# Two weight parts in conversion at once with a share for GpSimd, and attention normalised after the value product

## Chip, core and metric

The kernel runs on one core of a Trainium2 chip. The metric is the device time of one launch in microseconds (us). Besides the timed runs there is one profiled execution, from which every row below comes.

## What is computed

Attention over keys that are 4x4 means of `kv`, and then two feed-forward blocks one behind the other, all in float32 at the interface. The weights of the two blocks (`w_in`, `w_out`) arrive as 64-bit floats.

```python
kv_pool = kv.reshape(B, H // r, r, W // r, r, C).mean(axis=(2, 4))      # 768 keys per batch
k = v = kv_pool.reshape(B, -1, C) @ w_sr
s = scale * (q @ k.transpose(0, 2, 1)); s = s - s.max(-1, keepdims=True)
a = np.exp(s); a /= a.sum(-1, keepdims=True) + 1e-09
x = (a @ v)                                   # 2 x 12288 rows of 128
h = x @ w_in;  g = h * np.clip(h + 3.0, 0.0, 6.0) / 6.0;  x = g @ w_out     # d_ff 2048
h = x @ w_in2; g = h * np.cos(h);                         out = g @ w_out2
```

## The kernel before

**Blocks and units.** The 24576 rows are 48 blocks of 512. Per block there is one attention, and per feed-forward layer 8 units; a unit covers 256 of the 2048 hidden columns. The second layer runs LAG = 15 units behind the first, and the attention of a block is planned AHEAD = 3 units before the block's first unit.

**Precision.** Matrices are multiplied as three products of a high and a low float32r half. A unit's input pair is six matmuls of 512 columns on TensorE (lines 807 to 809), its output pair is six more (lines 815 to 817). Between them ScalarE and VectorE form the gate (line 822 then 825 in the first layer; 830, 833, 839 and 842 in the second), ScalarE rounds it to the high half (869) and GpSimd subtracts to get the low half (845). The two PSUM banks of an input pair come free when VectorE has done 825 or 842.

**Attention of a block.** The queries are transposed, by TensorE in the first BY_PE = 2 blocks (line 557, fp32), and through DRAM in the others. TensorE makes four score products (642), VectorE the row maxima (648), ScalarE the exponential with its row sums (654), VectorE one plus and one reciprocal on 128x1 (662, 665), and GpSimd scales the 768 weights of each row (669). In the first BY_PE blocks TensorE transposes the weights (725) and VectorE or ScalarE copies them out of PSUM (328, 330; the same copy helper). In the others VectorE parts the weights into 16-bit planes (697), SP stores them to DRAM (704) and loads them back transposed (740). Then come the value product (756), its high half on ScalarE (772) and its low half on VectorE (779); that pair is the input `x` of the first layer.

**Weights.** Each of the four matrices is converted from its 64-bit words in four parts, 16 in all (`plan_weight`). A part of 128x512 goes through ScalarE (358, 395) and seven VectorE operations: clamp 363, rebase 370, sign 377, power 383, rest 390, add 399, low 402. Its intermediate lies in one PSUM bank. TURNS = 1 lets one part at a time hold such a bank.

**Order.** Everything is written as operations with a priority and a planned cost; a list scheduler (`Plan.run`) picks for each free engine the ready operation with the lowest priority number and so fixes each engine's program. Weight part k of 16 has priority W_FIRST + W_STEP * k. Each engine and SP, which issues all DMAs, runs its program strictly in that order.

Of the kernel before, what the change touches and what calls it, by code (L numbers as in the profile page):

```python
# [16 lines left out]
ALU = mybir.AluOpType  # L17
# [16 lines left out]
AHEAD = 3  # L34
# [6 lines left out]
BY_PE = 2  # L41
# [3 lines left out]
TURNS = 1  # L45
# [12 lines left out]
W_FIRST, W_STEP = 10000.0, 4000.0  # L58
# [182 lines left out]
def attention_ffn_ffn_kernel(  # L241
# [45 lines left out]
    def tiles(tag, count, shape, dtype, pool=const):  # L287
# [15 lines left out]
            "scro": tiles("scro", NSCR, [C * 2, T], U16, dram),  # L303
            "scr": tiles("scr", NSCR, [NKC // 2, NJ * P * 2, 2 * P], U16, dram),
# [30 lines left out]
    def plan_weight(prio, n, src, part):  # L335
# [51 lines left out]
        def rest(e):  # L387

            t32 = work().bitcast(F32)
            nc.vector.scalar_tensor_tensor(  # L390
                out=t32, in0=words()[0], scalar=2.0**-52, in1=t32, op0=ALU.mult, op1=ALU.mult
            )
# [4 lines left out]
        def add(e):  # L397
            t32 = work().bitcast(F32)
            nc.vector.tensor_tensor(out=t32, in0=t32, in1=words()[1].bitcast(F32), op=ALU.add)

        def low(e):
            nc.vector.tensor_tensor(  # L402
                out=lo, in0=work().bitcast(F32), in1=hi.bitcast(F32), op=ALU.subtract
            )
# [8 lines left out]
        c = op(prio, {"dve": 602}, rest, [c])  # L413
        c = op(prio, {"dve": 602}, add, [c, a], drop=[raw])
        a = op(prio, {"dve": 602}, low, [c], drop=[tt, ("turn", n, part)])
# [127 lines left out]
    def plan_attention(prio, b):  # L543
# [73 lines left out]
        for j in range(NJ):  # L617
# [5 lines left out]
            scaled.append(a)  # L623
        acc, parts = ("xacc", b), []
# [7 lines left out]
        x_ready[1, b] = plan_split(prio + XS_AT, a, acc, ("x", 1, b), None)  # L632

    def plan_scores(prio, b, j, q_op, k_ops):
        ps, nm, e_, qt = ("s", b, j), ("nm", b, j), ("e", b, j), ("qt", b)
# [17 lines left out]
        def exp(e):  # L653
# [3 lines left out]
                accum_out=plan[nm][:, 1:2],  # L657
            )

        def inverse(e):  # L660
            t = plan[nm]
            nc.vector.tensor_scalar(
                out=t[:, 2:3], in0=t[:, 1:2], scalar1=1e-9, scalar2=None, op0=ALU.add
            )
            nc.vector.reciprocal(t[:, 3:4], t[:, 2:3])

        def normalize(e):
            t = flat(plan[e_])[:, 0:KEYS]
            nc.gpsimd.tensor_scalar(  # L669
                out=t, in0=t, scalar1=plan[nm][:, 3:4], scalar2=1.0, op0=ALU.mult, op1=ALU.mult  # L670
            )
# [7 lines left out]
            prio + 200, {"act": 1000}, exp, [a, *gate_exp(b)], take=[(e_, "w")], drop=[ps],  # L679
# [363 lines left out]
```

## Time and profile before

| | us |
|---|---|
| median of 3 runs | 2671.14 (2670.62 to 2671.53) |
| the profiled execution | 2667.97 |
| its span, first to last instruction | 2666.2 |

The profile gives busy time by engine, groups of instructions by line, the waits by the instruction that ended them, and a timeline. Matmuls are pipelined, so the time from one matmul's start to the next tells more than its own duration; on VectorE too an instruction's record overlaps the next by a little under 0.1 us. The granted clock is that of TensorE, 1.00 for full speed (2.4 GHz); half of that is its lower level.

### The profile page before, as it was taken

What the parts mean: (1) busy time and instruction counts of PE and PEld (TensorE: products, weight loads), DVE (VectorE), ACT (ScalarE), POOL (GpSimd) and SP (SyncE); (2) the same over time, 40 slices, a digit from 0 to 9 for tenths busy, and PEclk for the clock granted to TensorE, in tenths of its full rate; (3) what the DMA queues carried; (4) which work ended last, traced back from release to release, by engine and by line L of the source; (5) the groups of instructions that cost most, each with busy time, mean ns of one, the idle gap of its engine ahead of it and who ended that gap; (6) DMA issues with size and microseconds to landing.
All of it is one profiled execution on the core that took longest, in us unless ns stands there. A gap on an engine that the chain in (4) does not pass through costs nothing. (4 is left out here: it accounts for less than half of the span.)

```text
span 2666.2 us, 32082 instructions
## 1 busy us (share of the span) xinstructions
PE 2613.4 (98%) x11120; PEld 2064.6 (77%) x11120; DVE 2089.0 (78%) x2185; ACT 2299.1 (86%) x2613; POOL 2152.9 (81%) x1106
## 2 busy tenths in 40 slices
PE   7979999999999999999999999999999999999998
PEld 6657787778877877777777877787778777877787
DVE  8997787778777888877777777777777777777776
ACT  4888988888888888898889988998899888888887
POOL 1768888888888888788888888888888888888788
PEclk9989999999999999999999999999999999999999
DMA  6333334333433354433333343334332343234220
GB/s 191 101 84 77 87 91 104 75 88 89 105 72 91 87 139 111 111 76 89 97 83 87 78 104 85 91 75 100 91 91 72 103 92 91 72 99 91 71 60 28
DMA packets 516323, 241.77 MB, mean 91 GB/s; under 512 B 392256, under 2 KB 490688, under 8 KB 516160
## 3 DMA queue, kind: packets, MB, share of 16 engines
q1 hardware_dynamic: 516160, 239.72, 36.0%
q8 instruction: 87, 1.43, 0.2%
q14 instruction: 76, 0.62, 0.1%
HBM read 33.62 MB, written 109.31 MB: 54 GB/s over the span
## 5 line engine op out<-in xcount | busy, mean ns | idle before, releaser
L845 POOL TENSOR_TENSOR lo<-w,hi 128x1024 fp32r<-128x1024 f32 x768 | 1835.9, 2409 | 418.1 <-ACT hi L869 233.0
L869 ACT CAST hi<-w 128x1024 fp32r<-128x1024 f32 x768 | 793.2, 1051 | 111.3 <-DVE w L842 75.8
L807 PE MATMUL banks<-x,w_in_hi 128*128 128x512 f32 x1536 | 635.4, 414 | 19.5 <-DVE w L842 7.3
L815 PE MATMUL banks<-hi,w_out_hi 128*128 128x512 f32 x1536 | 629.5, 410 | 2.7 <-DVE w L825 2.3
L809 PE MATMUL banks<-x,w_in_hi 128*128 128x512 f32 x1536 | 603.1, 393 | 1.4 <-DVE x L779 1.4
L817 PE MATMUL banks<-lo,w_out_hi 128*128 128x512 f32 x1536 | 600.8, 391 | 2.2 <-POOL lo L845 2.2
L808 PE MATMUL banks<-x,w_in_lo 128*128 128x512 f32 x1536 | 602.0, 392 | 0.8 <-DVE w_in_lo L402 0.8
L816 PE MATMUL banks<-hi,w_out_lo 128*128 128x512 f32 x1536 | 599.3, 390 | 0.0
L842 DVE TENSOR_TENSOR w<-w,banks 128x1024 f32<-128x1024 f32 x384 | 465.2, 1217 | 143.9 <-ACT w L839 143.4
L825 DVE SCALAR_TENSOR_TENSOR w<-w,banks 128x1024 f32<-128x1024 f32 x384 | 462.6, 1216 | 117.3 <-ACT w L822 116.7
L833 DVE SCALAR_TENSOR_TENSOR w<-banks,w 128x1024 f32<-128x1024 f32 x384 | 466.0, 1219 | 108.4 <-ACT w L830 106.9
L822 ACT ACTIVATE w<-banks,three 128x1024 f32<-128x1024 f32 x384 | 423.6, 1118 | 43.3 <-PE banks L809 38.9
L839 ACT ACTIVATE w<-w 128x1024 f32<-128x1024 f32 x384 | 404.9, 1062 | 57.5 <-DVE w L833 55.3
L830 ACT ACTIVATE w<-banks 128x1024 int32<-128x1024 f32 x384 | 390.5, 1024 | 55.9 <-PE banks L809 53.5
L807 PEld LDWEIGHTS banks<-x,w_in_hi 128*128 128x128 f32 x1536 | 290.0, 189 | 119.4 <-DVE w L825 25.9
L815 PEld LDWEIGHTS banks<-hi,w_out_hi 128*128 128x128 f32 x1536 | 288.8, 188 | 79.0 <-issue 10.5
L697 DVE COPY w<-w 128x1536 uint16<-128x1536 uint16 x184 | 317.7, 1746 | 38.6 <-POOL w L669 38.4
L816 PEld LDWEIGHTS banks<-hi,w_out_lo 128*128 128x128 f32 x1536 | 288.8, 188 | 72.7 <-issue 17.2
L808 PEld LDWEIGHTS banks<-x,w_in_lo 128*128 128x128 f32 x1536 | 290.1, 189 | 70.1 <-issue 14.1
L809 PEld LDWEIGHTS banks<-x,w_in_hi 128*128 128x128 f32 x1536 | 289.8, 189 | 64.8 <-DVE x L779 1.8
L817 PEld LDWEIGHTS banks<-lo,w_out_hi 128*128 128x128 f32 x1536 | 288.4, 188 | 64.8 <-POOL lo L845 3.4
L756 PE MATMUL banks<-w,v_all 128*128 128x512 f32 x576 | 270.7, 593 | 0.0
(66 smaller groups left out, 1925.0 us busy)
## 6 DMA issues: line engine op xcount, KB each, us to landing
scr<-w SPq DMA_DIRECT2D x184, 384.0 KB, 2.5
w<-in_kv_dram SPq DMA_DIRECT2D x48, 256.0 KB, 5.0
w<-in_q_dram SPq DMA_DIRECT2D x48, 256.0 KB, 3.1
out_dram<-w SPq DMA_DIRECT2D x48, 256.0 KB, 2.0
scro<-w SPq DMA_DIRECT2D x47, 256.0 KB, 2.0
scrq<-w SPq DMA_DIRECT2D x46, 256.0 KB, 2.3
w<-in_moe_w_in_dram SPq DMA_DIRECT2D x8, 512.0 KB, 5.4
w<-in_moe_w_out_dram SPq DMA_DIRECT2D x8, 512.0 KB, 4.3
```

Of the source, the lines that this page charges most:

```text
L807: nc.tensor.matmul(t[:, i, :], w_hi[:, k, :], xx[:, 0, :], start=True, stop=False)
L808: nc.tensor.matmul(t[:, i, :], w_lo[:, k, :], xx[:, 0, :], start=False, stop=False)
L809: nc.tensor.matmul(t[:, i, :], w_hi[:, k, :], xx[:, 1, :], start=False, stop=True)
L815: nc.tensor.matmul(t, o_hi[:, k, :], h[:, i, :], start=(k == 0), stop=False)
L816: nc.tensor.matmul(t, o_lo[:, k, :], h[:, i, :], start=False, stop=False)
L817: nc.tensor.matmul(t, o_hi[:, k, :], l[:, i, :], start=False, stop=(k == 2 * NP - 1))
L822: nc.scalar.activation(plan[g], two(ps), AF.Relu, bias=three, scale=1.0)
L825: nc.vector.scalar_tensor_tensor(out=plan[g], in0=plan[g], scalar=6.0, in1=two(ps), op0=ALU.min, op1=ALU.mult)
L833: nc.vector.scalar_tensor_tensor(out=plan[g], in0=two(ps), scalar=0.25, in1=plan[g].bitcast(I32), op0=ALU.add, op1=ALU.subtract,)
L842: nc.vector.tensor_tensor(out=plan[g], in0=plan[g], in1=two(ps), op=ALU.mult)
L845: nc.gpsimd.tensor_tensor(out=plan[lo], in0=plan[g], in1=plan[hi].bitcast(F32), op=ALU.subtract)
L869: prio + HI_AT, {"act": 947}, lambda e: nc.scalar.copy(plan[hi], plan[g]), [a],
```

## The change

Four things at once.

1. The row sums of a block's four exponentials go to the four columns of one 128x4 tile. One plus and one reciprocal per block make their inverses. SP stores these to DRAM (`away`, 16 bytes per partition) and loads them back as one row copied to all 128 partitions (`back`). The weights stay unscaled: the 192 scalings by GpSimd (669) are gone. The value product, which has its rows along the free axis, is scaled by VectorE as it leaves PSUM; ScalarE rounds that, and GpSimd (not VectorE) subtracts for the low half (`plan_first`).
2. Two weight parts may be in conversion at once (TURNS 2), and for the first 8 of the 16 parts (`w_in1`, `w_out1`) the last two of the seven steps, add and low, are GpSimd's. The part's PSUM bank is then free after the fifth step.
3. Block 2 too is transposed by TensorE (BY_PE 3).
4. Attention is planned 4 units ahead instead of 3, and weight parts are spaced by 6000 instead of 4000 in priority.

```diff
-AHEAD = 3
+AHEAD = 4
-BY_PE = 2
+BY_PE = 3
-TURNS = 1
+TURNS = 2
+POOL_PARTS = 8
-W_FIRST, W_STEP = 10000.0, 4000.0
+W_FIRST, W_STEP = 10000.0, 6000.0
...
+        if by_pool:
+            c = op(prio, {"dve": 602}, rest, [c], drop=[tt, ("turn", n, part)])
+            c = op(prio, {"pool": 1250}, add, [c])
+            a = op(prio, {"pool": 1250}, low, [c, a], drop=[raw])
+        else:
...
-                accum_out=plan[nm][:, 1:2],
+                accum_out=plan[sm][:, j : j + 1],
...
+        def inverse(e):
+            t = plan[sm]
+            nc.vector.tensor_scalar(out=t, in0=t, scalar1=1e-9, scalar2=None, op0=ALU.add)
+            nc.vector.reciprocal(t, t)
+
+        def away(e):
+            nc.sync.dma_start(out=plan[scr].rearrange("(p j) -> p j", p=P), in_=plan[sm])
+
+        def back(e):
+            nc.sync.dma_start(
+                out=plan[row][:, 0, :],
+                in_=plan[scr].rearrange("(o t) -> o t", o=1).broadcast_to([P, T]),
+            )
...
+        def scaled(e):
+            t = plan[row]
+            nc.vector.tensor_tensor(
+                out=t[:, 1, :].rearrange("p (j q) -> p j q", j=NJ),
+                in0=one(acc).rearrange("p (j q) -> p j q", j=NJ),
+                in1=t[:, 0, :].rearrange("p (q j) -> p j q", j=NJ), op=ALU.mult,
+            )
+
+        def high(e):
+            nc.scalar.copy(plan[x][:, 0, :], plan[row][:, 1, :])
+
+        def low(e):
+            nc.gpsimd.tensor_tensor(
+                out=plan[x][:, 1, :], in0=plan[row][:, 1, :],
+                in1=plan[x][:, 0, :].bitcast(F32), op=ALU.subtract,
+            )
```

Line numbers move by up to 43. The order of the changed program differs nearly everywhere; three places follow.

VectorE while the first weight part is converted and the scores of blocks 0 and 1 come in (`w_80` is the part's raw words, `s_` the small tiles of the attention). Before:

```order
L370 TENSOR_SCALAR banks<-banks 128x512
L662 TENSOR_SCALAR s_114<-s_114 128x1
L665 RECIPROCAL s_114<-s_114 128x1
L377 SCALAR_TENSOR_TENSOR w_80<-w_80,banks 128x512
L662 TENSOR_SCALAR s_115<-s_115 128x1
L665 RECIPROCAL s_115<-s_115 128x1
L383 TENSOR_SCALAR banks<-w_80 128x512
L648 TENSOR_REDUCE s_116<-banks 128x1
L390 SCALAR_TENSOR_TENSOR banks<-w_80,banks 128x512
```

Now:

```order
L373 TENSOR_SCALAR banks<-banks 128x512
L366 TENSOR_SCALAR banks<-banks 128x512
L657 TENSOR_REDUCE s_116<-banks 128x1
L380 SCALAR_TENSOR_TENSOR w_80<-w_80,banks 128x512
L657 TENSOR_REDUCE s_117<-banks 128x1
L687 TENSOR_SCALAR s_113<-s_113 128x4
L688 RECIPROCAL s_113<-s_113 128x4
L386 TENSOR_SCALAR banks<-w_80 128x512
L333 COPY w_79<-banks 128x1024
L393 SCALAR_TENSOR_TENSOR w_80<-w_80,banks 128x512
```

One small pair stands for four, and steps of a second part (the second row) stand between those of the first.

GpSimd in the same stretch. Before, the scalings of the attention weights lead up to the first unit's low halves:

```order
L669 TENSOR_SCALAR w_79<-w_79,s_113 128x768
L669 TENSOR_SCALAR w_80<-w_80,s_114 128x768
L845 TENSOR_TENSOR lo_98<-w_89,hi_91 128x1024
L669 TENSOR_SCALAR w_79<-w_79,s_115 128x768
L845 TENSOR_TENSOR lo_99<-w_90,hi_92 128x1024
```

Now the last two steps of the weight parts do, with the low half of block 0's `x` (`x_107`) among them:

```order
L403 TENSOR_TENSOR w_82<-w_82 128x512
L407 TENSOR_TENSOR w_in_lo<-w_82,w_in_hi 128x512
L798 TENSOR_TENSOR x_107<-w_85,x_107 128x512
L403 TENSOR_TENSOR w_84<-w_84 128x512
L584 COPY w_82<-w_82 128x1024
L407 TENSOR_TENSOR w_in_lo<-w_84,w_in_hi 128x512
L403 TENSOR_TENSOR w_88<-w_88 128x512
L407 TENSOR_TENSOR w_out_lo<-w_88,w_out_hi 128x512
L887 TENSOR_TENSOR lo_98<-w_80,hi_91 128x1024
```

The scalings have left GpSimd's program and 16 weight steps have entered it ahead of the gates' low halves.

SP where a block's weights go through DRAM. Before:

```order
L704 DMA scr_128<-w_85 128x3x512
L704 DMA scr_128<-w_82 128x3x512
L549 DMA w_80<-in_q_dram 128x512
L740 DMA_TRANSPOSE w_86<-scr_128 128x2x1024
L740 DMA_TRANSPOSE w_88<-scr_128 128x2x1024
L740 DMA_TRANSPOSE w_85<-scr_128 128x2x1024
```

Now:

```order
L721 DMA scr_129<-w_86 128x3x512
L721 DMA scr_129<-w_79 128x3x512
L691 DMA scri_126<-s_114 128x4
L757 DMA_TRANSPOSE w_82<-scr_129 128x2x1024
L694 DMA w_85<-scri_126 128x512
L757 DMA_TRANSPOSE w_78<-scr_129 128x2x1024
L757 DMA_TRANSPOSE w_90<-scr_129 128x2x1024
```

The store of the inverse sums stands ahead of the three transposing loads, and the load of them between the first and the second.

## Rows read from the trace of the kernel before

**Rows 1.** The page: busy us, share of the span and instructions of each engine.
```profile
PE 2613.4 (98%) x11120; PEld 2064.6 (77%) x11120; DVE 2089.0 (78%) x2185; ACT 2299.1 (86%) x2613; POOL 2152.9 (81%) x1106
```

**Rows 2.** Busy time by stretch: PE, PEld, DVE, ACT, POOL, then PEclk, DMA share, GB/s.
```profile
34.24:60.95 26.71, 24.24 (x132) 19.70 (x133) 25.61 (x50) 18.83 (x33) 10.31 (x11) 1.00 0.25 48
60.95:100.00 39.05, 34.45 (x118) 23.54 (x118) 37.03 (x49) 29.02 (x34) 19.37 (x10) 0.91 0.43 109
100.00:160.00 60.00, 53.95 (x227) 41.92 (x225) 57.48 (x72) 53.48 (x61) 51.15 (x24) 0.98 0.31 88
160.00:220.00 60.00, 49.79 (x182) 37.03 (x183) 53.83 (x68) 45.53 (x56) 31.01 (x18) 0.91 0.29 70
220.00:2600.00 2380.00, 2371.38 (x10123) 1877.42 (x10122) 1850.16 (x1899) 2093.79 (x2363) 1986.35 (x1015) 1.00 0.37 90
```

**Rows 3.** Waits of PE, 34 to 220 us: us in total, times, longest.
```profile
PE banks L807 <- DVE w L842: 6.9, 3, 2.9
```

**Rows 4.** Timeline of DVE: start us, us, line, operation, out<-in [idle before <-releaser].
```profile
65.24 0.68 DVE L377 SCALAR_TENSOR_TENSOR w<-w,banks 128x512 int32<-128x512 int32 x1
65.83 0.15 DVE L662 TENSOR_SCALAR s<-s 128x1 f32<-128x1 f32 x1
...
66.10 0.68 DVE L383 TENSOR_SCALAR banks<-w 128x512 int32<-128x512 int32 x1
...
123.45 0.70 DVE L390 SCALAR_TENSOR_TENSOR banks<-w,banks 128x512 f32<-128x512 uint32 x1
124.18 0.70 DVE L399 TENSOR_TENSOR banks<-banks,w 128x512 f32<-128x512 f32 x1
```

**Rows 5.** DVE by line, 34 to 220 us: busy us, mean ns | idle before.
```profile
L648 DVE TENSOR_REDUCE s<-banks 128x1 f32<-128x768 f32 x17 | 16.1, 950 | 4.5 <-PE banks L642 4.4
L697 DVE COPY w<-w 128x1536 uint16<-128x1536 uint16 x8 | 14.0, 1745 | 1.0 <-POOL w L669 1.0
```

**Rows 6.** Timeline of DVE: the sixth product of the second layer.
```profile
155.38 1.22 DVE L842 TENSOR_TENSOR w<-w,banks 128x1024 f32<-128x1024 f32 x1
```

**Rows 7.** Timeline of PE: transposes of block 0's weights.
```profile
45.99 2.12 PE L725 MATMUL banks<-ident,w 128*128 128x128 f32 x16 [0.29 <-ACT w L654]
```

**Rows 8.** POOL by line, whole span.
```profile
L845 POOL TENSOR_TENSOR lo<-w,hi 128x1024 fp32r<-128x1024 f32 x768 | 1835.9, 2409 | 418.1 <-ACT hi L869 233.0 <-PE banks L817 113.4 <-issue 33.5
L669 POOL TENSOR_SCALAR w<-w,s 128x768 f32<-128x768 f32 x192 | 174.2, 916 | 44.1 <-DVE s L665 25.0 <-ACT hi L869 7.7 <-DVE s L662 5.5
L597 POOL TENSOR_TENSOR x<-w,x 128x512 fp32r<-128x512 f32 x46 | 59.9, 1302 | 5.5 <-ACT x L594 5.5
```

**Rows 9.** DMA issues: KB each, median us to landing.
```profile
scro<-w SPq DMA_DIRECT2D x47, 256.0 KB, 2.0
```

**Rows 10.** Timeline of SP, one block's transposing loads.
```profile
1269.27 6.67 SPq L740 DMA_TRANSPOSE w<-scr  x3
```

**Rows 11.** Timelines of PE, ACT and DVE: from the same block's last value product to its first unit.
```profile
1286.56 1.88 PE L756 MATMUL banks<-w,v_all 128*128 128x512 f32 x4
...
1290.01 0.68 PE L807 MATMUL banks<-x,w_in_hi 128*128 128x512 f32 x1
1290.53 0.39 PE L808 MATMUL banks<-x,w_in_lo 128*128 128x512 f32 x1
1290.76 0.40 PE L809 MATMUL banks<-x,w_in_hi 128*128 128x512 f32 x1
...
1288.47 0.59 ACT L772 CAST x<-banks 128x512 fp32r<-128x512 f32 x1 [0.59 <-PE banks L756]
...
1289.10 0.69 DVE L779 TENSOR_TENSOR x<-banks,x 128x512 fp32r<-128x512 f32 x1
```

**Rows 12.** Timelines: GpSimd continuously busy, GpSimd idle, and DVE within that idle time.
```profile
110.56 16.64 POOL L845 TENSOR_TENSOR lo<-w,hi 128x1024 fp32r<-128x1024 f32 x7 [0.59 <-DVE banks L399]
...
96.19 2.41 POOL L845 TENSOR_TENSOR lo<-w,hi 128x1024 fp32r<-128x1024 f32 x1 [12.86 <-PE banks L817]
...
91.56 0.70 DVE L399 TENSOR_TENSOR banks<-banks,w 128x512 f32<-128x512 f32 x1
```

More of the change, by code (lines that the diff above doesn't have):

```diff
@@ L390, in rest @@
             nc.vector.scalar_tensor_tensor(
-                out=t32, in0=words()[0], scalar=2.0**-52, in1=t32, op0=ALU.mult, op1=ALU.mult
+                out=words()[0].bitcast(F32) if by_pool else t32, in0=words()[0],
+                scalar=2.0**-52, in1=t32, op0=ALU.mult, op1=ALU.mult,
             )
@@ L397, in add @@
         def add(e):
[L398 to L399 removed]
+            t32 = (words()[0] if by_pool else work()).bitcast(F32)
+            ENG[e].tensor_tensor(out=t32, in0=t32, in1=words()[1].bitcast(F32), op=ALU.add)
         def low(e):
[L402 to L404 removed]
+            t32 = (words()[0] if by_pool else work()).bitcast(F32)
+            ENG[e].tensor_tensor(out=lo, in0=t32, in1=hi.bitcast(F32), op=ALU.subtract)
         a = op(prio, {"dma": 1560}, load, take=[(raw, "w")], spare=W_SPARE)
@@ L623, in plan_attention @@
             scaled.append(a)
+        row = plan_sums(prio + 1000 * NJ, b)
         acc, parts = ("xacc", b), []
@@ L678, in plan_scores, with plan_sums @@
         a = op(
-            prio + 200, {"act": 1000}, exp, [a, *gate_exp(b)], take=[(e_, "w")], drop=[ps],
-            table="exp",
+            prio + 200, {"act": 1000}, exp, [a, *gate_exp(b)],
+            take=[(e_, "w")] if j else [(e_, "w"), (sm, "s")], drop=[ps, nm], table="exp",
         )
         exps[b, j] = a
-        a = op(prio + 300, {"dve": 310}, inverse, [a])
-        return op(prio + 400, {"pool": 884}, normalize, [a], drop=[nm])
+        return a
+    def plan_sums(prio, b):
+        sm, row, scr = ("sm", b), ("row", b), ("scri", b)
+        def inverse(e):
[9 more added lines that the diff above has]
+            )
+        a = op(prio, {"dve": 310}, inverse, [exps[b, j] for j in range(NJ)], take=[(scr, "scri")])
+        a = op(prio + 100, {"dma": 500}, away, [a], drop=[sm])
+        return op(prio + 200, {"dma": 500}, back, [a], take=[(row, "w")], drop=[scr], spare=1)
     GK = NKC // 2
@@ L763, in plan_values, with plan_first @@
         )
+    def plan_first(prio, b, after, acc):
+        row, x = ("row", b), ("x", 1, b)
+        def scaled(e):
[12 more added lines that the diff above has]
+            )
+        a = op(prio, {"dve": 602}, scaled, after, drop=[acc])
+        a = op(prio + 100, {"act": 478}, high, [a], take=[(x, "x")])
+        return op(prio + 200, {"pool": 1230}, low, [a], drop=[row])
     def plan_split(prio, after, acc, x, s):
```

27 lines of the change are left out of this document (9 added, 18 removed).

## The prediction

> **What bounds the kernel now.** I read the page first, then busy time by stretch, then who ended TensorE's waits. TensorE is busy 98% of the span [rows 1], and the stretches say where the other 53 us are: between 220 and 2600 us it idles 8.6 of 2380 us at full clock, while VectorE, ScalarE and GpSimd each have over a tenth free [rows 2]. There the time is TensorE's own work, and the change takes none of that away. The loss is at the start. In the four stretches from 34.24 to 220 us TensorE idles 2.5, 4.6, 6.1 and 10.2 us, 23.3 in all. The granted clock is 0.91, 0.98 and 0.91 in the last three, below its full level behind those waits; busy time times the missing share is 3.1 + 1.1 + 4.5 = 8.7 us more. So 32 us can be won there, and half of that, 14.7, lies behind 160 us. In the same four stretches VectorE is busy 25.6 of 26.7, 37.0 of 39.1, 57.5 of 60 and 53.8 of 60 us: it carries the start, and the largest wait is an input pair that waits for VectorE's last step of the second layer [rows 3]. The first 34 us (means of `kv`) are the same in both kernels, and so is the end.
>
> **What the change takes from VectorE at the start.** Counted over the order up to the 26th first-layer gate and the 14th second-layer product, where before the last weight part is done.
> - Add and low of 8 parts: a 128x512 step occupies VectorE from 65.24 to 65.83, 0.59 us [rows 4]. 16 x 0.59 = 9.4 us less.
> - Small pairs: 16 before, 5 now. A pair takes 65.83 to 66.10, 0.27 us [rows 4]; 11 x 0.27 = 3.0 less.
> - Block 2: four plane copies fewer at 1.745 less some 0.09 of overlap [rows 5], 6.6 less; three more copies out of PSUM, which I price as the 1024-column step of 1.22 less overlap [rows 6], 3.4 more; one low half of the queries, 0.6 more. Net 2.6 less.
> - Steps that follow their own predecessor: 123.45 to 124.18 is 0.73 us instead of 0.59 [rows 4]. The order has 40 such pairs of neighbours before and 7 now, since two parts alternate: 33 x 0.14 = 4.6 less.
>
> Together about 20 us. The scaling of the product takes the place of the old low half (512 columns out of PSUM either way) and costs nothing new.
>
> **What it adds, and where it lies.** TensorE: 24 transposes of block 2 at 2.12/16 = 0.13 us [rows 7] are 3.1, four for its queries 0.5, and a few switches between fp32 and float32r (1290.01 to 1290.53 against the usual 0.23, so 0.3 each [rows 11]): 4.5 us. GpSimd: 16 x 1.30 = 21 us of weight steps and 48 x 1.30 = 62 us of low halves of `x`, against 192 x 0.916 = 176 us of scalings that go [rows 8]; it is busy 10.3 of the first 26.7 us of the start and 19.4 of the next 39.1 [rows 2], so the weight steps fit, though each part now waits for two steps of 1.30 instead of 0.59. ScalarE: at the start nothing changes but where its roundings read from; 29 scalings of the output by 0.6 us move to it from VectorE over the whole run, where both have room [rows 2].
>
> The DMAs: the trace has none of 16-byte pieces. The nearest row, 256 KB stored in runs, lands in 2.0 us [rows 9]; I take 2.0 each for `away` and `back`, with 0 (wholly covered) and 5 us each as bounds. On SP `away` now waits for the inverse ahead of the transposing loads, and `back` waits for `away` to land ahead of the second and third. One transposing load keeps SP 6.67/3 = 2.2 us [rows 10], which covers those 2.0. The three loads are issued by 1275.94 and the last value product starts at 1286.56 [rows 10, 11]: 10.6 us of cover, less landing, so even the upper bound hides. If it did not, TensorE would wait in the value product of each block.
>
> **Where the relief goes.** It does not all arrive, because the order also moves conversion forward. At the sixth product of the second layer, which ends at 156.6 us before [rows 6], VectorE has now all 96 of its conversion steps behind it instead of 82 (14 x 0.59 = 8.3 more), four more row maxima at 0.87 (3.5), three PSUM copies (3.4), one query half (0.6), one second-layer step (1.1), and nine small pairs fewer (2.4 less): 14.5 us more. Some 27 of the 33 neighbour pairs are saved by then, 3.8 us. So VectorE comes to that row 10.7 us **later** than before. TensorE has more behind it there: by the order four output pairs of the second layer (6 x 0.23 = 1.4 each), one input pair, two score products and the 4.5 us of transposes, against one input and two or three output pairs of the first layer. What is left for it is 3.5 to 10 us less than before; I take 7. From there on, before, 16.7 us are lost (the 14.7 behind 160, and 2 that I take of the 6.1 ahead of it). Now VectorE has 38 us of work up to the 14th product where before it had 52, and TensorE has over 50: TensorE leads, and only handovers cost. I take 3 us for these, between 0 and the old 16.7. Sum: +10.7 - 7 - 16.7 + 3 = **-10 us**. The extra transposes are inside the 7. Against the profiled execution that is 2668.0 - 10 = 2658; the median of the runs is 3.2 us above that execution, and the same step from it gives **2661 us**.
>
> **One rule of the skill.** VectorE's steps at 123.45 and 124.18 take 0.70 us each while GpSimd runs without a break from 110.56 to 127.2 [rows 4, 12]; the same step at 91.56 takes 0.70 with GpSimd idle for 12.86 us up to 96.19 [rows 12]. So work on GpSimd does not hold VectorE up there. The Trainium skill, Perfetto Trace Analysis, section "Optimizing Scalar/DVE Operations", warns that GpSimd and VectorE share an SBUF read port, so that moving work between the two might not help. No row shows it; its result is the fourth rival.
>
> **Rivals.**
> - *The early weights eat the relief.* TensorE waits ahead of the sixth product for what it no longer waits for behind it. For it: VectorE 10.7 us later there. Against it: second-layer work that is ready earlier. If the loss behind that row stays above 12 us, the sum is +1 to -1: 2671.
> - *More than forecast.* TensorE's remainder is 10 us smaller and no handover costs, and the early waits (13 us of idle ahead of 160) shrink too, by 6: -20, 2651.
> - *GpSimd in the chain to `x` (slower).* Before, the last value product is out at 1288.45, the low half is done at 1289.79, and its first user is the third matmul at 1290.76: 1 us to spare [rows 11]. Now the chain is 0.69 on VectorE, 0.59 on ScalarE, 1.30 on GpSimd and handovers, 2.7 us, and by the order one output pair more (1.4 us) stands between. Again 1 us to spare. But if a low half of a gate, 2.41 us [rows 8], has just begun on GpSimd, up to 1.4 us are missing. At 0.22 us a block over 45 blocks the forecast gain is gone; at 0.5 us the kernel takes 22 - 10 = +12: 2683. Against it: 394 of 2380 us on GpSimd are free [rows 2], and a planned order puts the split where GpSimd should be free.
> - *The port.* Each of GpSimd's 16 weight steps stops VectorE for its 1.30 us: +20.8 - 10 = +11, 2682. The rows above speak against it.
>
> **How the numbers follow.** Forecast 0.61, with its own range 2654 to 2667; early weights 0.17; more 0.12; chain to `x` 0.07; port 0.03. The range 2647 to 2673 holds the forecast, the first rival and half of the second. This kernel can be told from no change at about 0.2%, 5.3 us. Faster by more: nine tenths of the forecast, the second rival, little else, 0.69. Within: 0.19. Slower: the last two and a little of the first, 0.12.
>
> **What would show it.** In the changed profile: VectorE's work between 34 and 220 us lower, its sixth second-layer product near 167 us, the last weight step ahead of it; TensorE's idle time and low clock between 160 and 220 nearly gone; the stretch from 220 on at its old rate, with no wait for the scaled product or GpSimd's low half of `x`; `away` and `back` landing in about 2 us. A wait of TensorE for GpSimd in each block, or VectorE idle at the scaling, would make it wrong, as would idle time that has moved ahead of 160 us instead of vanishing.

## Result: 32 us faster, three times the forecast

| | before | after |
|---|---|---|
| median of 4 runs, us | 2671.34 (2670.62 to 2671.97) | 2639.39 (2638.53 to 2642.41) |
| profiled execution, us | 2667.97 | 2639.83 |
| its span, us | 2666.2 | 2637.8 |

The ratio is 0.9883, 95% interval 0.9865 to 0.9900. The time lies below the forecast's range (2647 to 2673), and below the second rival, "more than forecast" (2651). The page's line on the engines, after, beside [rows 1]:

```profile
PE 2599.3 (99%) x11148; PEld 2070.3 (78%) x11148; DVE 2031.0 (77%) x1852; ACT 2295.6 (87%) x2642; POOL 2055.5 (78%) x976
```

The stretches of the changed kernel, with the columns of [rows 2] (span, then busy time and instructions of PE, PEld, DVE, ACT and POOL, PEclk, DMA share, GB/s):

```profile
34.24:60.95 26.71, 23.46 (x131) 18.14 (x130) 24.59 (x38) 17.81 (x33) 7.38 (x7) 1.00 0.19 48
60.95:100.00 39.05, 32.61 (x121) 22.90 (x120) 37.60 (x50) 32.59 (x40) 33.24 (x21) 0.96 0.42 118
100.00:160.00 60.00, 58.00 (x256) 45.10 (x255) 57.98 (x75) 51.18 (x63) 46.38 (x23) 1.00 0.21 58
160.00:220.00 60.00, 59.92 (x260) 47.88 (x259) 52.03 (x47) 53.63 (x64) 43.45 (x22) 1.00 0.45 113
...
1400.00:2000.00 600.00, 600.00 (x2578) 480.90 (x2577) 455.25 (x409) 535.24 (x612) 477.93 (x225) 1.00 0.40 96
2000.00:2600.00 600.00, 600.00 (x2573) 480.19 (x2573) 451.77 (x404) 534.86 (x606) 479.65 (x223) 1.00 0.35 83
```

And the last two of these stretches in the kernel before:

```profile
1400.00:2000.00 600.00, 598.25 (x2555) 473.98 (x2555) 464.94 (x480) 530.35 (x597) 503.17 (x258) 1.00 0.36 89
2000.00:2600.00 600.00, 598.84 (x2557) 474.71 (x2556) 462.75 (x477) 528.55 (x594) 499.05 (x253) 1.00 0.34 83
```

From 160 to 220 us TensorE's idle time falls from 10.2 us [rows 2] to 0.1 and the clock is full: the forecast gain is there. But look at the steady stretches. TensorE's busy time there grows by 1.75 and 1.16 us, 0.3% and 0.2%, while the matmuls in brackets grow by 23 and 16, 0.9% and 0.6%. Something was gained that the busy column does not show.

**A measure that shows it.** Each kernel has 9216 feed-forward matmuls. The start of the 800th, and the time from there to the last, part the run into the start (with all of the weights' conversion) and the steady part. From the two profiled executions (that of the kernel before is 3.4 us below its median, that of the changed kernel 0.4 above, so the two gains add up to 28.7 us and not to 32):

| | 800th starts at | from there to the last |
|---|---|---|
| before | 316.1 | 2343.7 |
| after | 302.8 (13.3 less) | 2328.3 (15.4 less) |

The prediction forecast 10 us for the start and nothing for the steady part. So the question is where those 15.4 us come from.

**Where the steady time was lost.** TensorE in the kernel before, a first-layer input pair (start us, us, line, out<-in, idle before):

```profile
322.28 0.39 PE L808 MATMUL banks<-x,w_in_lo 128*128 128x512 f32 x1
322.50 0.40 PE L809 MATMUL banks<-x,w_in_hi 128*128 128x512 f32 x1
323.20 0.50 PE L807 MATMUL banks<-x,w_in_hi 128*128 128x512 f32 x1 [0.30 <-DVE w L825]
323.54 0.39 PE L808 MATMUL banks<-x,w_in_lo 128*128 128x512 f32 x1
```

Matmuls usually start 0.227 us apart, but each record is 0.39 long. Here a matmul starts 0.70 after the one ahead of it, since VectorE frees the bank late, and the next one 0.34 later: 0.59 us lost, of which the row shows 0.30 as idle. A stall below 0.16 us shows nothing at all. (The Trainium skill, Perfetto Trace Analysis, section "Tensor Engine Instruction (MATMUL, LD_WEIGHTS)", says that the end of a matmul in the profile is estimated from its size and not observed; the rows here show only that the records overlap.) I counted the distances over 0.25 us from a feed-forward matmul to the next one, leaving out those right behind a value product, from the 800th to the 9000th: 129 before, worth 22.2 us above 0.227, of which 8.4 show as idle; 35 after, worth 8.4, of which 4.3 show. That is 13.8 of the 15.4 us.

Who is late is mostly VectorE: of the 129, 38 (12.1 us) end within 0.2 us of a VectorE step that releases them, and 31 more (4.1 us) follow a stall directly; 2 (0.8 us) end with ScalarE, and for the other 58, all short (5.2 us), the trace names nobody. VectorE has waits of its own from 310 to 2600 us (in all, times, longest). Before:

```profile
DVE s L662 <- ACT w L654: 50.1, 78, 1.4
DVE w L697 <- POOL w L669: 34.5, 30, 2.1
```

After, the plane copies' waits:

```profile
DVE w L714 <- issue: 5.5, 32, 0.4
DVE w L714 <- ACT w L663: 1.3, 3, 0.7
```

Before, VectorE stood 50 us ahead of the small pair (waiting for the row sum of the exponential) and 35 us ahead of the plane copies (waiting for GpSimd's scaling). What stands behind them in its row, the gates that free TensorE's banks, waited too. The change takes both waits away. That alone does not explain the gain: e1 and e4 below have neither wait and keep a steady part of 2341.4 and 2340.4. Nor does VectorE wait less in total: for ScalarE at the gates (825, 833 and 842, now 867, 875 and 884) it waits 433 us where it waited 339. What counts is which gate stands behind a wait.

### The profile page after: what moved, and what is told of

Same layout as the page of the kernel before. It is cut to its first block, busy times and chain, and to the rows that moved or that the text cites. A ratio compares the mean times of both kernels' runs of the same rounds, so it can differ in the third digit from the quotient of the medians.

```text
span 2637.8 us, 32119 instructions
## 1 busy us (share of the span) xinstructions
PE 2599.3 (99%) x11148; PEld 2070.3 (78%) x11148; DVE 2031.0 (77%) x1852; ACT 2295.6 (87%) x2642; POOL 2055.5 (78%) x976
## 5 line engine op out<-in xcount | busy, mean ns | idle before, releaser
L911 ACT CAST hi<-w 128x1024 fp32r<-128x1024 f32 x768 | 781.2, 1056 | 46.7 <-DVE w L884 32.5
L849 PE MATMUL banks<-x,w_in_hi 128*128 128x512 f32 x1536 | 621.5, 405 | 9.7 <-DVE w L867 4.8
L851 PE MATMUL banks<-x,w_in_hi 128*128 128x512 f32 x1536 | 600.2, 391 | 0.0
L864 ACT ACTIVATE w<-banks,three 128x1024 f32<-128x1024 f32 x384 | 420.0, 1120 | 24.8 <-PE banks L851 24.5
L849 PEld LDWEIGHTS banks<-x,w_in_hi 128*128 128x128 f32 x1536 | 288.4, 188 | 90.1 <-DVE w L884 12.1
L850 PEld LDWEIGHTS banks<-x,w_in_lo 128*128 128x128 f32 x1536 | 288.4, 188 | 67.1 <-issue 11.4
L714 DVE COPY w<-w 128x1536 uint16<-128x1536 uint16 x180 | 310.3, 1746 | 8.1 <-issue 5.5
```

The costliest lines, as they stand in the source:

```text
L849: nc.tensor.matmul(t[:, i, :], w_hi[:, k, :], xx[:, 0, :], start=True, stop=False)
L850: nc.tensor.matmul(t[:, i, :], w_lo[:, k, :], xx[:, 0, :], start=False, stop=False)
L851: nc.tensor.matmul(t[:, i, :], w_hi[:, k, :], xx[:, 1, :], start=False, stop=True)
L864: nc.scalar.activation(plan[g], two(ps), AF.Relu, bias=three, scale=1.0)
L911: prio + HI_AT, {"act": 947}, lambda e: nc.scalar.copy(plan[hi], plan[g]), [a],
```

## Experiments

Medians of the runs; the kernel before was 2670.6 to 2671.0 beside them. "800th" and "steady" are the two columns of the table above, from each run's profile. The profiled execution of the kernel before is 3 us below its median, so the columns show less of a gain than the medians. Some expectations measure the steady part to the 9000th matmul (2292.6 before, 2277.3 after). A single profiled execution can lie some 3 us beside its median: e1's is 1.5 above.

| | us | ratio (95%) | 800th | steady |
|---|---|---|---|---|
| before | 2671.34 | | 316.1 | 2343.7 |
| after | 2639.39 | 0.9865 to 0.9900 | 302.8 | 2328.3 |
| e1 product alone | 2661.98 | 0.9954 to 0.9979 | 314.1 | 2341.4 |
| e2 weights alone | 2664.56 | 0.9969 to 0.9987 | 318.0 | 2339.2 |
| e3 AHEAD 4 alone | 2671.16 | 0.9993 to 1.0011 | 320.7 | 2342.9 |
| e4 after, AHEAD 3 | 2653.11 | 0.9921 to 0.9946 | 304.7 | 2340.4 |
| e5 product and AHEAD 4 | 2650.22 | 0.9908 to 0.9935 | 314.3 | 2328.2 |
| e6 after, BY_PE 2 | 2646.95 | 0.9897 to 0.9924 | 307.3 | 2329.5 |
| e7 after, AHEAD 5 | 2665.47 | 0.9971 to 0.9988 | 309.4 | 2345.8 |
| e8 after, no weight step on GpSimd | 2650.01 | 0.9907 to 0.9934 | 314.2 | 2328.0 |
| e9 after, small pairs back | 2660.03 | 0.9945 to 0.9970 | 311.0 | 2340.2 |
| e10 after, GpSimd's pass back | 2717.30 | 1.0159 to 1.0187 | 326.3 | 2383.3 |
| e11 after, TURNS 1 | 2655.62 | 0.9928 to 0.9953 | 322.9 | 2324.4 |
| e12 after, W_STEP 4000 | 2650.73 | 0.9911 to 0.9936 | 313.9 | 2328.5 |
| e13 after, GpSimd's pass aside | 2640.19 | 0.9871 to 0.9898 | 305.8 | 2327.1 |
| e14 e10 with AHEAD 3 | 2672.63 | 0.9997 to 1.0014 | 309.6 | 2353.7 |
| e15 after, row without a stride | 2726.98 | 1.0193 to 1.0225 | 324.3 | 2398.4 |

### The change taken apart (e1 to e5)

e1, the changed code with

```diff
-AHEAD = 4
+AHEAD = 3
-BY_PE = 3
+BY_PE = 2
-TURNS = 2
+TURNS = 1
-POOL_PARTS = 8
+POOL_PARTS = 0
-W_FIRST, W_STEP = 10000.0, 6000.0
+W_FIRST, W_STEP = 10000.0, 4000.0
```

> Only the product is normalised in place of the weights (inverse sums by way of DRAM); the weight conversion, AHEAD, BY_PE and W_STEP stay as in the kernel before. Theory A (the trace of the changed kernel shows about 16 us gained ahead of 300 us and 12 to 13 us gained little by little behind it; A says that the second share comes from the scalings that leave GpSimd and the small VectorE steps that leave the steady part, and has nothing to do with the conversion): about 12 us faster than before, near 2659, and the gain grows with the blocks, none of it ahead of 220 us. Rival B (the second share comes from AHEAD = 4, which moves the attention of a block ahead of one unit more): within 4 us of before, 2667 to 2673. Rival C (the second share comes from the late weights, whose conversion still disturbs the order): within 4 us of before too.

e2, the kernel before with the changed `plan_weight` and

```diff
-TURNS = 1
+TURNS = 2
+POOL_PARTS = 8
-W_FIRST, W_STEP = 10000.0, 4000.0
+W_FIRST, W_STEP = 10000.0, 6000.0
```

> Only the conversion of the weights is changed: two parts at once, eight parts with GpSimd's add and low, 6000 between the parts; scores are still normalised by GpSimd, AHEAD = 3 and BY_PE = 2. Theory A: the gain of the start without that of the steady part, some 12 to 17 us faster than before, 2654 to 2659, with the number of matmuls per microsecond behind 300 us as before. Rival C (conversion also gives the steady share): 25 us or more faster, 2646 or less. Prediction's reading (relief of VectorE is 20 us but the early weights eat half): 10 us or less, 2661 or more, since the pairs that the normalisation saves at the start are missing here.

e3, the kernel before with

```diff
-AHEAD = 3
+AHEAD = 4
```

> The kernel before with AHEAD = 4 in place of 3 and nothing else: the attention of a block is planned one unit earlier. Theory A: within 4 us of before, 2667 to 2675. Rival B: about 12 us faster, near 2659, by a higher matmul rate behind 300 us.

e4, the changed kernel with

```diff
-AHEAD = 4
+AHEAD = 3
```

> The changed kernel with AHEAD = 3 as before; everything else of the change stays. Theory A: within 4 us of the changed kernel, 2636 to 2644. Rival B: loses the steady share, about 2651. A third reading (the longer way through DRAM needs the unit more of lead): TensorE waits for the scaled product in each block, 0.2 to 0.5 us by 47 blocks, 2648 to 2662.

No theory fits all four. The product alone gains 9 us, but its trace shows 2.3 in the steady part where theory A wants 12. The weights alone gain 6 and AHEAD alone nothing, so B in its plain form falls. Yet AHEAD decides in the changed kernel: with 3, the steady part is 2340.4. That asks for the product and AHEAD 4 without the conversion, e5 (e1 with AHEAD 4):

```diff
-AHEAD = 3
+AHEAD = 4
```

> The product normalised in place of the weights, together with AHEAD = 4; the weight conversion and BY_PE as in the kernel before. So far: the product alone 2662, AHEAD = 4 alone 2671, the changed kernel with AHEAD = 3 2653 and with 4 2639. Theory D (the small stalls of the steady part go only where the small VectorE steps are gone and the attention is planned one unit earlier; this has nothing to do with the conversion): 11 to 14 us below the product alone, 2648 to 2651, with fewer than 40 of the 0.25 to 0.6 us gaps between first-layer matmuls behind 310 us, where the kernel before has about 99. Rival E (AHEAD = 4 pays only because the conversion is out of the way early in the changed kernel): within 4 us of the product alone, 2658 to 2666.

2650.22, and a steady part of 2328.2, the changed kernel's to 0.1 us, with 33 of the long distances counted above. From 329 us on, each engine's program in e5 is that of the changed kernel, instruction for instruction. Theory D holds: the 15 us of the steady part come from the product together with AHEAD 4, and the conversion has no share in it. Of the 32 us, 20.6 are in e5, and 10.8 come on top by conversion and BY_PE.

VectorE's waits, 310 to 2600 us, suggest why neither half does it alone. In e1 (product, AHEAD 3):

```profile
DVE x L825 <- ACT x L816: 40.3, 34, 1.2
DVE w L714 <- ACT w L663: 20.5, 23, 1.0
```

There the plane copies (714) wait for the exponential itself; e4 has 21.5 us of it, the changed kernel 1.3. In e3 (AHEAD 4 alone) the small pair still waits 31.4 us and the plane copies 27.9 for the scaling.

### Which wait it was (e9, e10, e13, e14)

e9, in the changed `plan_scores`:

```diff
-            take=[(e_, "w")] if j else [(e_, "w"), (sm, "s")], drop=[ps, nm], table="exp",
+            take=[(e_, "w")] if j else [(e_, "w"), (sm, "s")], drop=[ps], table="exp",
...
+        def pair(e):
+            t = plan[nm]
+            nc.vector.tensor_scalar(
+                out=t[:, 2:3], in0=t[:, 0:1], scalar1=1e-9, scalar2=None, op0=ALU.add
+            )
+            nc.vector.reciprocal(t[:, 3:4], t[:, 2:3])
+        op(prio + 300, {"dve": 310}, pair, [a], drop=[nm])
```

> The changed kernel with the two small VectorE steps put back behind each exponential (an add and a reciprocal on 128x1, as before, planned at 310 ns; their result is used by nothing). All else stays, GpSimd's relief too. So far: product alone 2662, product with AHEAD = 4 2650, and by the traces the 8200 feed-forward matmuls from the 800th on take 2292.6 us before, 2277.2 with product and AHEAD = 4, 2277.3 in the changed kernel. Theory V (the steady share of 15 us comes from VectorE, which was late with the gates that free TensorE's banks): the steady part goes back to about 2290 us, and with up to 3 us at the start the time is 2650 to 2656. Theory G (it comes from GpSimd, whose scaling no longer stands between the exponential and the planes): steady part at 2277 to 2280, time within 4 us of the changed kernel, 2638 to 2643.

Theory V: the steady part goes back by 11.9 us, to 2340.2, and the start by 8.2. The time, 2660.0, is above V's range, since the start loses more than the 3 us that I allowed. Small as the two steps are (VectorE by line, whole span of e9),

```profile
L685 DVE RECIPROCAL s<-s 128x1 f32<-128x1 f32 x192 | 31.6, 164 | 6.6
L682 DVE TENSOR_SCALAR s<-s 128x1 f32<-128x1 f32 x192 | 27.8, 145 | 0.0
```

these 59 us of VectorE, spread over 2650, cost 20 us of the kernel, together with the order that the scheduler makes of them: from 1310 us on TensorE and GpSimd run the changed kernel's order, but VectorE and ScalarE have some gates exchanged behind the small steps. No run has the steps without that. They hardly wait here (6.6 us of idle time ahead of them); in the kernel before, the same steps waited 50 us.

e10, behind the exponential, with a `unit` of ones:

```diff
+        def by_one(e):
+            t = flat(plan[e_])[:, 0:KEYS]
+            nc.gpsimd.tensor_scalar(
+                out=t, in0=t, scalar1=unit[:, 0:1], scalar2=1.0, op0=ALU.mult, op1=ALU.mult
+            )
+        return op(prio + 400, {"pool": 884}, by_one, [a])
-        return a
```

> The changed kernel with GpSimd's pass over the weights put back (a multiplication by one, the same instruction of some 0.9 us, 192 of them, between the exponential and the planes); the small VectorE steps stay away. Theory G: the steady part goes back to about 2290 us, and at the start the 32 passes of the first blocks collide with GpSimd's weight steps: the time is 2655 to 2665. Theory V: steady part at 2277 to 2280 us; only the start loses, by up to 11 us (what the weight steps on GpSimd are worth): 2642 to 2651.

2717, 78 us more than the changed kernel and worse than G's range. The largest wait of TensorE, 310 to 2600 us, then the one of VectorE that is new:

```profile
PE banks L857 <- DVE w L875: 33.4, 27, 2.5
```

```profile
DVE w L722 <- POOL w L683: 56.7, 45, 2.0
```

From 1376 us on there is one such wait in each block. One of them in the timelines of GpSimd, VectorE and TensorE (722 is the plane copy, 683 the pass, 895 a low half, 695 the add of the inverse sums, 875 the first layer's gate, 883 a step of the second layer's):

```profile
1438.88 0.92 POOL L683 TENSOR_SCALAR w<-w,unit 128x768 f32<-128x768 f32 x1
...
1444.27 2.42 POOL L895 TENSOR_TENSOR lo<-w,hi 128x1024 fp32r<-128x1024 f32 x1
```

```profile
1439.83 1.75 DVE L722 COPY w<-w 128x1536 uint16<-128x1536 uint16 x1 [1.10 <-POOL w L683]
1441.50 1.21 DVE L875 SCALAR_TENSOR_TENSOR w<-w,banks 128x1024 f32<-128x1024 f32 x1
1442.63 0.95 DVE L658 TENSOR_REDUCE s<-banks 128x1 f32<-128x768 f32 x1
1443.50 1.74 DVE L722 COPY w<-w 128x1536 uint16<-128x1536 uint16 x1
1445.16 1.57 DVE L695 TENSOR_SCALAR s<-s 128x4 f32<-128x4 f32 x1
1446.76 0.18 DVE L696 RECIPROCAL s<-s 128x4 f32<-128x4 f32 x1
1446.86 1.20 DVE L883 SCALAR_TENSOR_TENSOR w<-banks,w 128x1024 f32<-128x1024 f32 x1
1447.97 1.21 DVE L875 SCALAR_TENSOR_TENSOR w<-w,banks 128x1024 f32<-128x1024 f32 x1
```

```profile
1447.72 0.39 PE L867 MATMUL banks<-lo,w_out_hi 128*128 128x512 f32 x1
1449.24 0.50 PE L857 MATMUL banks<-x,w_in_hi 128*128 128x512 f32 x1 [1.13 <-DVE w L875]
```

VectorE stands 1.10 us for the pass, then shows no idle time for 9 us, and its last gate ends at 1449.18; TensorE starts 0.06 later, 1.3 us later than it could. A delay of VectorE becomes one of TensorE at the gate seven instructions on. (That an engine takes its instructions strictly in their order is also what the Trainium skill, Perfetto Trace Analysis, says of VectorE, ScalarE and GpSimd in the section "Tensor Engine Instruction (MATMUL, LD_WEIGHTS)".)

The wait for the pass is not the only delay in these 9 us. The add of the inverse sums (695), four values per partition, lasts 1.57 us and ends at 1446.73; GpSimd's low half ends at 1446.69. By line, after and then e10:

```profile
L687 DVE TENSOR_SCALAR s<-s 128x4 f32<-128x4 f32 x48 | 12.4, 259 | 0.0
```

```profile
L695 DVE TENSOR_SCALAR s<-s 128x4 f32<-128x4 f32 x48 | 76.7, 1597 | 2.3 <-ACT w L664 2.3
```

All 14 runs that have this add, the changed kernel among them, show the same: with GpSimd idle it takes 0.15 to 0.18 us (one of 672 is longer), and when it starts while GpSimd works it ends within 0.1 us of the end of a GpSimd instruction. In the changed kernel 5 of 48 meet GpSimd, in e10 46. No other step of VectorE shows this, and the 128x1 adds of the kernel before never take over 0.16 us. So e10 does two things at once: 57 us of waits for the pass, and 64 us more in this add. In the block shown, the last gate without the 1.41 us of hold would end at 1447.77 (an estimate from these rows), before TensorE's turn at 1447.95. Earlier in the run, up to 946 us, the add is held as long and no stall follows it within 6 us. The kernel before had the pass and not this add, so e10 does not tell what its scalings cost.

But some 55 us in the steady part are more than the kernel before ever lost there, and GpSimd's own time was a suspect. e13 lets the same pass run on a tile that nobody else uses:

```diff
-            t = flat(plan[e_])[:, 0:KEYS]
+            t = aside
-        return op(prio + 400, {"pool": 884}, by_one, [a])
+        op(prio + 400, {"pool": 884}, by_one, [a])
+        return a
```

> GpSimd's pass of 0.9 us put back as in the run before last, 192 times, but on a tile of its own that nothing else reads or writes: GpSimd has the same work, and no engine waits for it. It costs GpSimd 176 us, and the low halves of the gates come later by it. If the 55 us of the steady part that the pass in the chain cost come from GpSimd's time: 2700 or more again. If they come from VectorE, which stands still in its queue until the pass has ended, with the gates that TensorE waits for behind it: the steady part stays at 2277 to 2282 us, and only the start loses, up to 10 us: 2640 to 2652.

GpSimd by line, the pass in e10 and in e13:

```profile
L683 POOL TENSOR_SCALAR w<-w,unit 128x768 f32<-128x768 f32 x192 | 175.6, 919 | 58.6 <-ACT w L664 58.6
```

```profile
L684 POOL TENSOR_SCALAR aside<-aside,unit 128x768 f32<-128x768 f32 x192 | 175.7, 915 | 5.0
```

The same 176 us on GpSimd, and 2640.2 in place of 2717.3, the changed kernel's time within its runs. From 1216 us on the order is the changed kernel's too, and the add of the inverse sums takes 11.8 us in all. GpSimd's work beside the path costs nothing; the same work in the path costs 77 us, by VectorE's waits for it, by the held adds and by the order that follows from it, and no run parts the three. And the place decides the size, e14 (e10 with AHEAD 3 in place of 4):

```diff
-AHEAD = 4
+AHEAD = 3
```

> GpSimd's pass in the chain (multiplication by one between the exponential and the planes) with AHEAD = 3 in place of 4. The kernel before had this pass and AHEAD = 3, and lost 15 us in its steady part, not 55. If the 1.2 us that TensorE waits in each block come from where AHEAD = 4 puts the plane copies ahead of a second-layer gate: the steady part is 2285 to 2300 us and the time 2660 to 2680. If the pass costs 55 us at any place: 2700 or more.

2672.6, as expected, with 2302.3 us to the 9000th matmul, just above the expected 2285 to 2300. Its waits of VectorE and TensorE, 310 to 2600 us:

```profile
DVE w L722 <- POOL w L683: 79.7, 35, 3.2
```

```profile
PE banks L857 <- DVE w L875: 4.1, 4, 2.5
```

VectorE stands longer than in e10 (79.7 us against 56.7) and its small add still takes 47.5 us in all, but TensorE's wait is an eighth: the gates that it needs next stand elsewhere in the row. So what a delay of VectorE costs depends on what the order puts behind it, and AHEAD moves that. It can be read as the reason why AHEAD 4 is worth 12 us with the product, 0 without it, and why 5 loses 17 in the steady part (e7):

```diff
-AHEAD = 4
+AHEAD = 5
```

> The changed kernel with AHEAD = 5. If what AHEAD = 4 gave is more lead for the product's way through DRAM, a further unit gives little or nothing: 2637 to 2642. If it gave a better place of the attention between the units by chance of the order, the step can go either way by as much as it did from 3 to 4 (14 us): 2626 to 2654. It holds one block more of tiles, so a lack of tiles would show as waits of SP's loads and of ScalarE: slower, over 2645.

2665.47, above the 2626 to 2654 that a place by chance allowed; whether tiles were lacking was not looked into. Its waits of TensorE, 310 to 2600 us:

```profile
PE banks L857 <- DVE x L825: 6.2, 5, 1.8
PE banks L849 <- DVE w L867: 4.4, 6, 1.6
```

TensorE waits for VectorE in other places (825 forms the second layer's `x`). Part of e7's loss lies behind held adds: 8 of them in the steady part are held, 13.8 us in all, and 11.3 of its 24.5 us of long distances (counted as above) lie within 6 us behind them; in the changed kernel 2 are held, with 1.0 of 8.4 us behind them. Beyond that, why 4 is the good place, and not 3 or 5, no run settles.

### The start (e6, e8, e11, e12)

Each undoes one setting of the changed kernel.

```diff
-BY_PE = 3
+BY_PE = 2
```

> The changed kernel with BY_PE = 2: the third block's weights are turned by way of DRAM and not by TensorE, as before. The prediction priced the third block on TensorE at 3.6 us of TensorE work and a gain of 6.6 less 3.4 less 0.6 = 2.6 us on VectorE. If TensorE leads from 160 us on, that work is lost time and this kernel is 2 to 4 us faster, 2635 to 2638. If VectorE still leads there, its plane copies come back: 2640 to 2648. If the stores of planes hold back the early weights: over 2648.

```diff
-POOL_PARTS = 8
+POOL_PARTS = 0
```

> The changed kernel with no weight step on GpSimd (add and low of all parts on VectorE; two parts still at once). VectorE gets 16 steps of 0.59 us more at the start, 9.4 us. If VectorE carries the start as the prediction says and takes the relief in full: 2647 to 2650. If half of the relief is lost to the earlier conversion, as the prediction says: 2642 to 2646. If GpSimd's steps are no gain since each part waits for two steps of 1.30 us: 2639 or less. The rate behind 300 us should not change by any of these.

```diff
-TURNS = 2
+TURNS = 1
```

> The changed kernel with TURNS = 1: one part of weights in conversion at a time, as before; GpSimd keeps its share of eight parts. The prediction priced the two parts at once with 33 neighbour pairs of VectorE by 0.14 us, 4.6 us. If that is all: 2643 to 2645. If one part at a time also makes the next part wait for its bank and its turn until the last VectorE step: more, 2648 to 2656. If GpSimd's share alone carries the start (the part's turn ends ahead of the two GpSimd steps): within 2 us of the changed kernel.

```diff
-W_FIRST, W_STEP = 10000.0, 6000.0
+W_FIRST, W_STEP = 10000.0, 4000.0
```

> The changed kernel with the parts of weights 4000 apart in the plan, as before, so that conversion is drawn forward still more. First rival of the prediction (the early weights eat what the relief gives): the time goes up by as much as VectorE is later at the first units, 2644 to 2652. If early conversion costs nothing, since TensorE makes it up behind: 2637 to 2642.

They cost 7.6, 10.6, 16.2 and 11.3 us, most of it ahead of the 800th matmul (4.5, 11.4, 20.1 and 11.1). The sum is 46 us, but all four together bring 10.8 over e5: they don't add. The other three without GpSimd's share (e8) bring nothing over e5 (2650.0 and 2650.2); the other three without two parts at once (e11) are 5 us worse than e5. TensorE's largest waits from 34 to 220 us, in e11:

```profile
PE banks L849 <- DVE w L884: 5.7, 3, 4.4
PE banks L849 <- DVE w L867: 3.9, 4, 1.5
```

in the changed kernel:

```profile
PE banks L849 <- DVE w L867: 4.8, 6, 1.0
PE banks L651 <- DVE w L867: 2.9, 2, 2.5
```

With one turn, the wait of [rows 3] for the second layer's last step (884, was 842) is back. The conversion alone on the old normalisation (e2) brings its 800th matmul no earlier at all (its 6 us lie behind that, and what they come from was not looked into): there GpSimd has the scalings of the first blocks beside the weight steps and is busy 49.9 of the first 65.8 us of the start, against 40.6 in the changed kernel (that this is the reason was not tested apart).

### The row without a stride (e15)

```diff
-            nc.sync.dma_start(out=plan[scr].rearrange("(p j) -> p j", p=P), in_=plan[sm])
+            nc.sync.dma_start(out=plan[scr].rearrange("(j p) -> p j", p=P), in_=plan[sm])
...
-                out=t[:, 1, :].rearrange("p (j q) -> p j q", j=NJ),
-                in0=one(acc).rearrange("p (j q) -> p j q", j=NJ),
-                in1=t[:, 0, :].rearrange("p (q j) -> p j q", j=NJ), op=ALU.mult,
+                out=t[:, 1, :], in0=one(acc), in1=t[:, 0, :], op=ALU.mult,
```

> The changed kernel with the inverse sums stored in the order of the product's columns (pieces of 4 bytes in place of 16), so that VectorE reads its row of 512 without a stride. In the trace the scaled product takes 1.076 us with the stride, while a 128x512 step from a bank takes 0.68: 48 x 0.39 = 19 us less on VectorE, 0.4 us a block. If VectorE's time in its queue is what the steady part still pays (two small steps of 1.1 us a block cost 12 us there): 2 to 5 us faster than the changed kernel, 2634 to 2638. If only waits count and not this step, which stands where TensorE has work: 2638 to 2641. If the store of 512 pieces of 4 bytes lands after the last value product (it has some 10 us of cover): slower, 2645 or more.

The scaled product by line, after and then e15:

```profile
L788 DVE TENSOR_TENSOR w<-banks,w 128x512 f32<-128x512 f32 x48 | 51.7, 1076 | 0.1
```

```profile
L788 DVE TENSOR_TENSOR w<-banks,w 128x512 f32<-128x512 f32 x48 | 32.7, 681 | 6.5 <-DMA w<-scri 4.7 <-PE banks L773 1.8
```

DMA issues (KB each, median us to landing), after and then e15, and TensorE's largest wait in e15:

```profile
w<-scri SPq DMA_DIRECT2D x48, 256.0 KB, 4.3
...
scri<-s SPq DMA_DIRECT2D x48, 2.0 KB, 2.8
```

```profile
scri<-s SPq DMA_DIRECT2D x48, 2.0 KB, 12.1
```

```profile
PE banks L773 <- DMA w<-scr: 38.3, 31, 2.9
```

VectorE's step falls from 1.076 to 0.681 us as expected, and the kernel loses 88 us with every engine's order as in the changed kernel. The same 2 KB in 512 pieces of 4 bytes land in 12.1 us in place of 2.8. `back` waits on SP for that, and the transposing loads stand behind `back`: TensorE waits for the transposed weights 31 times. This is the way by which the prediction said that the two DMAs could hurt (`away` and `back` ahead of the loads, 10.6 us of cover), reached at 12.1 us.

## Why the prediction was wrong, step by step

- **"There the time is TensorE's own work, and the change takes none of that away": this step failed**, and with it the 15.4 us that the runs show in the steady part. It read 8.6 idle us of 2380 in [rows 2]. Matmul records overlap (0.39 us long, 0.227 apart), so a stall shows only beyond 0.16 us. The text ahead of the prediction even says that the distance of starts tells more than a duration; the argument then used busy time. By the distance of starts TensorE lost 22.2 us there in stalls, and the product with AHEAD 4 takes 13.8 of them away (e5 has the same steady part).
- **VectorE "has over a tenth free": true and beside the point.** It was late at single gates. The prediction saw the small pairs only as 0.27 us of work and only at the start (3.0 us); put back, with the order that follows, they cost 8.2 there and 11.9 behind it (e9). The 192 scalings were booked as GpSimd's relief; e13 shows that this much of GpSimd's time is free. What VectorE's waits for them cost in the kernel before is not shown, since e10 holds up the new add as well.
- **AHEAD 4 was not priced** apart from what the order moved at the start. In the steady part it is worth 12 us beside the product (2340.4 to 2328.3) and nothing alone (2343.7 to 2342.9).
- **The start: right in mechanism, near in size, in part by luck.** 10 us forecast; the 800th matmul comes 13.3 earlier. The sixth second-layer product was to end near 167 us and ends at 173.0, 16.4 later than before and not 10.7. With that and no handovers the prediction's own sum gives 13.3 only if TensorE's remainder is 13.0 and not 7 (its range was 3.5 to 10); no run takes this apart. As forecast, the loss behind 160 us went (10.2 us of idle time to 0.1). The last weight step lies ahead of that product, as forecast (it starts at 149.64 us, in the kernel before at 212.96). VectorE after, in two places:

```profile
149.64 0.69 DVE L407 TENSOR_TENSOR w_out_lo<-banks,w_out_hi 128x512 fp32r<-128x512 f32 x1
...
171.82 1.21 DVE L884 TENSOR_TENSOR w<-w,banks 128x1024 f32<-128x1024 f32 x1
```

  The term that was too high is the 3 us for handovers behind it: TensorE idles 0.1 us there.
- **First rival, "the early weights eat the relief": it came and was paid back.** The 240th feed-forward matmul starts 9.1 us later than before, the 400th 16.7 earlier. e12 was to draw the weights forward still more and loses 11 us, but its last weight step starts at 165.85 us, 16 us behind the changed kernel's, so it does not test this rival.
- **Second rival, "more than forecast":** its parts sum to -22 and not to -20, 2649 in place of 2651. It came nearest, but it looked for the extra gain at the start alone.
- **The terms of the relief.** GpSimd's share, 9.4 us: 10.6 by e8. Two parts at once, 4.6 us: 16.2 by e11. Block 2 on TensorE, between 2.6 gained on VectorE and 3.6 spent on TensorE: 7.6 gained by e6. They were added as if independent, and are not.
- **"The scaling costs nothing new": wrong by 0.39 us a block**, 1.076 us in place of 0.69, for the row with a stride of 16 bytes. The Trainium skill, SBUF — State Buffer, section "Door 1: The DMA port swizzle", says that SBUF has lines of 16 bytes and that each access to a new line pays; e15, where the stride is gone and the step takes 0.681, agrees. No run shows a wait that it cost; e15 changes the store too and can't price it.
- **The DMAs: 2.0 us each forecast, 2.8 and 4.3 measured**, inside the bounds of 0 to 5, and hidden: no wait of VectorE for `back` in the changed kernel (0.1 us of idle time ahead of 788).
- **Third rival, GpSimd in the chain to `x`: did not come.** The profile shows no wait of TensorE for `x` behind 310 us.
- **Fourth rival, the port: did not come for the weight steps, but another step is held.** VectorE and GpSimd after, at the same time:

```profile
69.61 0.69 DVE L380 SCALAR_TENSOR_TENSOR w<-w,banks 128x512 int32<-128x512 int32 x1
70.20 0.70 DVE L366 TENSOR_SCALAR banks<-banks 128x512 f32<-128x512 f32 x1
70.81 0.69 DVE L386 TENSOR_SCALAR banks<-w 128x512 int32<-128x512 int32 x1
```

```profile
68.89 1.31 POOL L407 TENSOR_TENSOR w_out_lo<-w,w_out_hi 128x512 fp32r<-128x512 f32 x1
```

  GpSimd's weight step runs from 68.89 to 70.20, and VectorE's steps start 0.59 to 0.61 us apart, as in [rows 4]. But the add of the inverse sums, which the change brings in and the prediction counts as a small step of 0.27 us with its reciprocal, does wait for GpSimd's instruction to end: 5 of 48 in the changed kernel, 0.6 to 1.9 us long, 46 in e10. The steps that the prediction compared in [rows 4 and 12] work in PSUM (390 and 399). That the port is the reason is not shown apart.

**Open.** Why AHEAD 4 and not 3 or 5; and how the 15 us share out between the pair and the scaling in the kernel before, since either costs another sum in another order (e9, e10, e14). How e10's 77 us share out between the wait for the pass and the held add. No version tried beats the changed kernel. e11's steady part is 3.9 us shorter, but only since 24 score matmuls (4.2 us) lie ahead of its 800th matmul and not behind it.

## What to carry to other kernels

Where one engine is 98% busy, take its rate from the distance of its starts, not from its idle time: records that overlap hide stalls, here 14 us of them. An instruction that is late on an in-order engine costs what stands behind it, so on the engines that free buffers look at the idle time ahead of small steps, and at their length too: a step of 0.16 us that takes 1.6 is being held, and no idle time shows it. 176 us of GpSimd work were free beside the path; in the path they cost 77 us. And settings that act on the same queue don't add: undoing four of them one by one cost 46 us where together they had brought 11.

## What the runs showed of the hardware

- A store of 2 KB to DRAM lands in 2.8 us as 128 pieces of 16 bytes and in 12.1 as 512 of 4.
- VectorE's 128x512 product from a bank takes 0.681 us with its other operand in a row, and 1.076 with that operand at a stride of 16 bytes.
- When a matmul starts 0.6 us or more behind the one ahead of it, the next one follows 0.34 us later, not 0.227 (all 20 such places in the steady part of the kernel before): such a stall costs some 0.11 us more than its wait.
- VectorE's add of 128x4 float32 takes 0.16 us with GpSimd idle; when it starts while a GpSimd instruction runs, it ends with that one or a later one, up to 4.2 us long (e10). The 128x1 adds of the kernel before and the 128x512 weight steps that work in PSUM don't show this.
- GpSimd's plain addition of 128x512 (the weights' add) takes 1.04 us, not the 1.30 that the prediction took from the subtraction that writes float32r.
